# Attention and gated MLP on one core: attention's pieces ahead of erf's batch, and one weight conversion behind the first copy of h

## Chip, cores and metric

The kernel runs on one core of a Trainium2 chip. The metric is the time of one execution on the device in microseconds (us); before the change it is 989.19 us, the median of three runs (986.95 to 989.7).

## What is computed

Linear attention with an RMS norm, followed by a two-layer MLP whose activation is h times erf(softplus(h)):

```python
kv = einsum('bhsd,bhse->bhde', k, v)          # k^T v for every head
out = einsum('bhsd,bhde->bhse', q, kv)
x = out / sqrt(mean(out * out, axis=-1) + 1e-6) * g_norm
h = x @ w_in                                   # x: 4608 x 512, w_in: 512 x 2048
g = h * erf(softplus(h))
result = g @ w_out                             # w_out: 2048 x 512
```

There are 8 batches of 8 heads, 576 rows and 64 columns; the heads of a batch side by side form the 512 columns of x. q, k, v and the result are float32. w_in and w_out come as float64, and the kernel takes their bits apart and makes float32 of them.

## The kernel before

**Groups and steps.** The 4608 rows are cut into nine groups of 512: eight hold 512 rows of one batch each, and the ninth the last 64 rows of all eight. The first two groups (T = 0 and 1) are computed with plain float32 matmuls, while the weights are converted and cut into three parts for the later groups. These go through 16 steps each, one for every 128 columns of w_in (n counts the steps, f is the step within the group). The later groups, from about 275 us on, are not touched by the change.

**A step of the first two groups** issues, in this order: the first list of attention's pieces for the next group (steps[f][0]); a conversion of weights when one is due (weights(): split, join, load); the product of an earlier h with its activation (L584, DVE); four matmuls of h (h_ps, L588, PE; each shows as two records), which take one of two PSUM banks in turn; the copy of h out of PSUM (L599, ACT) and softplus (L600, ACT); in every fourth step erf over the last four tiles (L613, ACT) and a load of softplus's table; the second list of attention's pieces (steps[f][1]); and the product with w_out for the tile five steps back (project, o_ps, L468, PE). Each engine runs its instructions in the order in which they were issued, and waits at the head of its queue until the operands of the next one are there; the order is written out by hand.

**Attention's pieces** for one pair of heads (p = 0 to 3) of the next group: products (k^T v into kv_ps L276 and the transposed q into qt_ps L298 on PE; bd_kv and the tail copied by DVE, L291 and L294; qT copied by ACT, L299); apply (kv_ps L303 and se_ps L304 on PE, then their square by ACT, L307); mean (ms_ps L330 on PE, then Ln, Exp and Square on ACT, L337 to L339, with a load of the table of exp and ln before them and of softplus's after); norm (L345, L348, L357 on DVE). They share two PSUM banks ("at"): kv_ps of a pair takes the bank that L345 of the pair before reads, qt_ps the one that L357 reads. While group 0 is in its steps, products stand in steps 3, 6, 9 and 12, apply in 4, 7, 10 and 13, mean in 5, 8, 11 and 14, all in the second list. Erf's batches stand in steps 3, 7, 11 and 15. While group 1 is in its steps, no piece of the second list falls on a step with erf's batch.

**A conversion** is a split (two DVE instructions, L194 and L203, and two ACT instructions, a relu L202 and an identity L206) and a join (three DVE instructions, L213, L217, L227). Before step 0, attention for group 0 runs in rounds, and w_rounds says which conversions lie between them; a conversion covers two tiles, apart from the first two. The round at the end splits the fifth and sixth tile of w_in (numbers 4 and 5), which are joined in step 2.

Of the kernel before, what the change touches and what calls it, by code (L numbers as in the profile page):

```python
# [28 lines left out]


# [1 line left out]

# [17 lines left out]
BATCH = 4  # L50
# [7 lines left out]
def kernel(  # L58
# [17 lines left out]
    NP = H // 2  # L76
# [24 lines left out]
    def exp_ln_table():  # L101
        nc.scalar.preload_act_table_set("natural_log_exp_and_others")

    def softplus_table():
        nc.scalar.preload_act_table_set("softplus")  # L105
# [131 lines left out]
    def w_next(what):  # L237
        i = w_at[what]
        if i < len(w_order):
            w_at[what] = i + 1  # L240
            {"load": load_w, "split": w_split, "join": w_join}[what](*w_order[i][1:])

    def weights():

        w_next("split")
        w_next("join")
        w_next("load")
# [4 lines left out]
    def attention(T, p, pools=None):  # L252
# [6 lines left out]
        def bank(name):  # L259
            pool, tag = (pools or {}).get(name, (ps_at, "at"))  # L260
            return pool.tile([P, G], FP32, name=name, tag=tag)

        def square_tile(name):

            if T == 0:
                return gate.tile([P, G], FP32, name=name, tag="h")
            return attp.tile([P, G], FP32, name=name, tag="qT")
# [49 lines left out]
            nc.vector.tensor_copy(out=hi, in_=sq)  # L317
            nc.vector.tensor_tensor(out=lo, in0=sq, in1=hi.bitcast(FP32), op=ALU.subtract)

        def mean():  # L320
            ms = st["ms"] = bank("ms_ps")
            if T >= FIRST:


                nc.tensor.matmul(ms, lhsT=mean_w, rhs=st.pop("hi"), start=True, stop=False)
                nc.tensor.matmul(ms, lhsT=mean_w, rhs=st.pop("lo"), start=False, stop=True)
                u = square_tile("u")
            else:
                u = st.pop("qT")
                nc.tensor.matmul(ms, lhsT=mean_f, rhs=u, start=True, stop=True)  # L330
            if T > 0:
                r = attp.tile([P, G], FP32, name="rms_r", tag="rms_r")
                exp_ln_table()
            else:
                r = gate.tile([P, G], FP32, name="rms_r", tag="s")
            st["u"], st["r"] = u, r
            nc.scalar.activation(r, ms, AF.Ln, bias=eps_col)  # L337
            nc.scalar.activation(r, r, AF.Exp, scale=-0.5)
            nc.scalar.activation(u, r, AF.Square)  # L339
            if T > 0 or p == NP - 1:  # L340
                softplus_table()

        def norm():
# [100 lines left out]
    def w_upper(which, f):  # L444

        t = stage.tile([P, 3, G], FP32R, name="w_new", tag="w_new")
        if which == "in":
            x, parts = w_in_sb[:, :, f * P : f * P + P], t.rearrange("p i (c f) -> p i c f", c=KC)
        else:
            x, parts = w_out_sb[:, f, :], t  # L450
        upper_w(x, parts[:, 0])
        w_new[which, f] = t, x, [parts[:, i] for i in range(3)]

    def w_lower(which, f):
        t, x, parts = w_new.pop((which, f))
        lower_w(x, *parts)
        kept = w_kept[which, f] = dram.tile([P, 3, G], FP32, name=f"w_{which}{f}")
        nc.sync.dma_start(out=kept, in_=t.bitcast(FP32))
# [5 lines left out]
    def project(f, g, last):  # L464
        for j in range(J):
            if f == 0:
                o_ps[j] = ps_o.tile([P, DM], FP32, name=f"o_ps{j}", tag=f"o{j}")
            nc.tensor.matmul(  # L468
                o_ps[j],
                lhsT=g[:, j * P : j * P + P],  # L470
                rhs=w_out_sb[:, f, :],
                start=(f == 0),
                stop=last,
            )
# [12 lines left out]
    def sums():  # L487

        for j in range(J):
            e = es[j] = acc.tile([P, DM], FP32, name="e", tag="e")  # L490
            if j % 2:
                nc.scalar.copy(e, o_ps[j])
            else:
                nc.vector.tensor_copy(out=e, in_=o_ps[j])

    def unit(name):
        return gate.tile([P, G], FP32, name=name, tag=name[0])


    for _ in range(2):  # L500
# [7 lines left out]
        2: ("join", "load", "split"),  # L508
        3: ("join", "load"),
        5: ("split",),  # L510
        6: ("join", "load", "split"),
    }
    banks_0 = {"kv_ps": (ps_at, "at"), "qt_ps": (ps_h, "h"), "ms_ps": (ps_h, "h")}
    first = [attention(0, p, banks_0 | {"se_ps": (ps_o, f"o{p}")}) for p in range(NP)]
# [20 lines left out]
    def load_parts(which, n):  # L535

        pool = w_in_p if which == "in" else w_out_p
        for _ in range(n):
            if w_seq[which]:
                key = w_seq[which].pop(0)  # L540
                t = pool.tile([P, 3, G], FP32, name=f"w_{which}_parts", tag="w")
                nc.sync.dma_start(out=t, in_=w_kept[key])
                w_now.setdefault(key, []).append(t)


    def pieces_of(T):


        steps = [([], []) for _ in range(FC)]
        for p in range(NP):  # L550
            products, apply, halve, mean, norm, split = attention(T, p)
            short = T < FIRST or p == NP - 1
            f = (BATCH - 1) * (p + 1) if T < FIRST else BATCH * p
            steps[f][1].append(products)
            steps[f + 1][1].append(apply)
            steps[f + 2][0].append(halve)
            steps[f + 3 - short][short].append(mean)
            steps[f + 4 - short][0].append(norm)
            steps[f + 5 - 2 * short][0].append(split)
        return steps  # L560
# [4 lines left out]
    for n in range(FIRST * FC + 1):  # L565
        T, f = divmod(n, FC)
        if n == FC:
            early_room.close()
            late = ctx.enter_context(tc.tile_pool(name="late", bufs=1))
            x_new = ctx.enter_context(tc.tile_pool(name="x_new", bufs=1))  # L570
            acc = ctx.enter_context(tc.tile_pool(name="acc", bufs=J))
            stage_room = ctx.enter_context(ExitStack())
            stage = stage_room.enter_context(tc.tile_pool(name="stage", bufs=5))
            x_forms[FIRST] = late.tile([P, 3, KC, G], FP32R, name="x_forms0")
        if T < FIRST:
            if f == 0:
                steps = pieces_of(T + 1)
            for piece in steps[f][0]:
                piece()
        while w_at["join"] < len(w_order) and w_order[w_at["join"]][0] <= n + 2:  # L580
            weights()
        done = n - LAG + 1
        if 0 <= done < whole:
            nc.vector.tensor_tensor(out=hs[done], in0=hs[done], in1=ss[done], op=ALU.mult)  # L584
        if T < FIRST:
            h_ps = ps_h.tile([P, G], FP32, name="h_ps", tag="h")
            for c in range(KC):
                nc.tensor.matmul(  # L588
                    h_ps,
                    lhsT=w_in_sb[:, c, f * P : f * P + P],  # L590
                    rhs=xT[T][:, c, :],
                    start=(c == 0),
                    stop=(c == KC - 1),
                )
            if n == whole:
                old_h = wide.tile([P, BATCH, G], FP32, name="h", tag="h")
            h = hs[n] = old_h[:, n - whole] if n >= whole else unit("h_sb")
            s = ss[n] = unit("s_sb")
            nc.scalar.copy(h, h_ps)  # L599
            nc.scalar.activation(s, h, AF.Softplus)  # L600
            for key in list(w_new):
                w_lower(*key)
            if T == FIRST - 1:
                for key in to_cut[:2]:
                    w_upper(*key)
                if not w_new and stage_room is not None:
                    stage_room.close()
                    stage_room = None
                    w_in_p = ctx.enter_context(tc.tile_pool(name="w_in_p", bufs=BATCH))
                    load_parts("in", BATCH)  # L610
            if f % BATCH == BATCH - 1:
                for i in range(n - BATCH + 1, n + 1):
                    nc.scalar.activation(ss[i], ss[i], AF.Erf)  # L613
                softplus_table()
            for piece in steps[f][1]:
                piece()
            if T == FIRST - 1:
                for key in to_cut[2:3]:
                    w_upper(*key)
                del to_cut[:3]  # L620
        if n >= LAG:
            T2, f2 = divmod(n - LAG, FC)
            last = n - LAG in (FC - 1, whole - 1)
            project(f2, hs[n - LAG], last)
            if last:
                sums()
                if T2 == 0:
                    for j in range(J):
                        store(T2, j, es.pop(j))
# [41 lines left out]
    for m in range(first_batch, batches + 1):  # L671
        T, b = divmod(m, NB)
# [7 lines left out]
        def piece():  # L680
            if todo:
                todo.pop(0)()
# [79 lines left out]
```

## Time and profile before

| | before |
|---|---|
| time, median of 3 | 989.19 us |
| span of the profiled execution | 985.3 us |
| PE busy | 947.6 us (96%) |
| DVE busy | 732.9 us (74%) |
| ACT busy | 618.1 us (63%) |
| ACT table loads | 45, 57.7 us |
| DMA, mean rate | 264 GB/s |
| PE waits for DMA v_sb at L276, at the start | 7.8 us in three waits |

PE is TensorE's matmuls, PEld its weight loads, DVE VectorE, ACT ScalarE, SP SyncE, which issues most transfers. The page gives busy shares over the whole span; the waits view adds up the idle time of an engine by what ended it; the timeline lists instructions in order of time; the chain of waits goes back from the last instruction to what released it. The granted clock of PE is 1.00 where PE runs at full speed. A busy share says little where stages have different limits: what a moved instruction is worth is read at the wait that ends last in its stage.

### The profile page before, as it was taken

To read this page: it belongs to the slowest core of one execution; us is meant where nothing else is said; L and a number is where in the kernel's file an instruction comes from. 1 tells how busy PE (TensorE), PEld (TensorE's weight loads), DVE (VectorE), ACT (ScalarE), POOL (GpSimd) and SP (SyncE) were. 2 spreads that over 40 slices of the span, in tenths; PEclk is the share of its full clock that TensorE was granted. 3 is DMA by queue.
4 is the path that set the end of the run, shared out by engine and by line. 5 is a ranking of instruction groups with operands and counts; after the bars stand their busy time and mean duration, and the time that the engine had idled before them with its cause. 6 is when DMAs were issued, how large, how long until landed. Compare 5 with 4: busy or idle time off the path is not lost.

```text
span 985.3 us, 11734 instructions
## 1 busy us (share of the span) xinstructions
PE 947.6 (96%) x4328; PEld 679.1 (69%) x4328; DVE 732.9 (74%) x1039; ACT 618.1 (63%) x822; POOL 2.4 (0%) x10
## 2 busy tenths in 40 slices
PE   6799899999999999999999999999999999989996
PEld 4344444444477877787778787878787787768885
DVE  3987675766367777787777777788777788786666
ACT  4888665777465666666666666666666666665550
POOL 0000000000000000000000000000000000000000
PEclk9999999999999999999999999999999999999999
DMA  9855405888379985998699878988796679667942
GB/s 277 251 179 180 142 17 217 311 353 331 128 269 348 379 281 201 323 360 298 223 278 369 302 263 254 370 297 279 239 339 246 246 258 347 238 229 286 364 199 75
DMA packets 100936, 259.76 MB, mean 264 GB/s; under 512 B 44048, under 2 KB 57360, under 8 KB 100880
## 3 DMA queue, kind: packets, MB, share of 16 engines
q1 hardware_dynamic: 99248, 256.73, 73.3%
q10 hardware_dynamic: 1568, 2.29, 0.8%
q8 instruction: 34, 0.56, 0.2%
q14 instruction: 22, 0.18, 0.1%
q0 software_dynamic: 64, 0.00, 0.0%
HBM read 224.40 MB, written 34.60 MB: 263 GB/s over the span
## 4 chain that ended last, share of the span: by engine, by line
PE 76%; DVE 14%; ACT 6%; DMA 2%; issue 2%; SPq 0%; DVEq 0%
PE n_ps L431 33%; PE m_ps L431 16%; PE h_ps L588 9%; PE o_ps L468 9%; DVE h L724 3%; PE se_ps L304 3%; DVE e L416 2%; PE qt_ps L298 2%; PE kv_ps L276 1%; DVE x L357 1%; DVE u L348 1%; DVE e L411 1%; DVE h L416 1%; DVE u L345 1%; DMA w_raw<-in_moe_w_in_dram 1%
## 5 line engine op out<-in xcount | busy, mean ns | idle before, releaser
L431 PE MATMUL n_ps<-x_forms,w_in_parts 128*128 128x512 f32 x896 | 233.3, 402 | 3.0 <-ACT x_forms L382 2.7
L431 PE MATMUL n_ps<-w_out_parts,g_forms 128*128 128x512 f32 x928 | 232.7, 393 | 3.3 <-DMA w_out_parts<-w_out 3.3
L431 PEld LDWEIGHTS n_ps<-w_out_parts,g_forms 128*128 128x128 f32 x928 | 175.2, 189 | 41.5 <-DMA w_out_parts<-w_out 4.5
L431 PEld LDWEIGHTS n_ps<-x_forms,w_in_parts 128*128 128x128 f32 x896 | 166.6, 188 | 47.3 <-issue 9.1
L708 ACT ACTIVATE s<-h 128x512 f32<-128x512 f32 x112 | 71.1, 635 | 200.3 <-DVE h L416 200.3
L431 PE MATMUL m_ps<-w_out_parts,g_forms 128*128 128x512 f32 x464 | 125.2, 392 | 0.0
L588 PE MATMUL h_ps<-xT,w_in_sb 128*128 128x512 f32 x256 | 115.2, 593 | 5.1 <-ACT h_sb L599 2.2
L431 PE MATMUL m_ps<-x_forms,w_in_parts 128*128 128x512 f32 x448 | 120.0, 390 | 0.0
L416 DVE TENSOR_TENSOR h<-m_ps,h 128x512 f32<-128x512 f32 x112 | 77.1, 688 | 50.5 <-ACT h L706 47.1
L385 DVE TENSOR_TENSOR g_forms<-h,g_forms 128x1024 fp32r<-128x1024 f32 x58 | 70.9, 1223 | 47.0 <-ACT g_forms L382 46.7
L468 PE MATMUL o_ps<-w_out_sb,h_sb 128*128 128x512 f32 x224 | 101.8, 598 | 0.0
L431 PEld LDWEIGHTS m_ps<-w_out_parts,g_forms 128*128 128x128 f32 x464 | 88.1, 190 | 18.6
L431 PEld LDWEIGHTS m_ps<-x_forms,w_in_parts 128*128 128x128 f32 x448 | 84.1, 188 | 17.6
L588 PEld LDWEIGHTS h_ps<-xT,w_in_sb 128*128 128x128 f32 x256 | 48.3, 190 | 65.7 <-issue 56.2
L416 DVE TENSOR_TENSOR e<-m_ps,e 128x512 f32<-128x512 f32 x116 | 80.3, 692 | 17.5 <-PE m_ps L431 9.6
L411 DVE SCALAR_TENSOR_TENSOR e<-n_ps,e 128x512 f32<-128x512 f32 x88 | 60.3, 685 | 27.4 <-PE n_ps L431 27.4
L468 PEld LDWEIGHTS o_ps<-w_out_sb,h_sb 128*128 128x128 f32 x224 | 42.6, 193 | 50.7 <-issue 49.1
L706 ACT ACTIVATE h<-n_ps 128x512 f32<-128x512 f32 x112 | 65.6, 585 | 17.1 <-PE n_ps L431 17.0
L386 DVE SCALAR_TENSOR_TENSOR g_forms<-g_forms 128x1024 fp32r<-128x1024 f32 x58 | 71.1, 1225 | 2.0
L382 ACT ACTIVATE g_forms<-h 128x1024 fp32r<-128x1024 f32 x58 | 61.2, 1055 | 7.8 <-DVE h L724 6.4
L724 DVE TENSOR_TENSOR h<-h,s 128x1024 f32<-128x1024 f32 x56 | 65.9, 1219 | 0.0
L105 ACT ACT_TABLE_LOAD x45 | 57.7, 1283 | 0.8
(81 smaller groups left out, 946.4 us busy)
## 6 DMA issues: line engine op xcount, KB each, us to landing
w_out_parts<-w_out SPq DMA_DIRECT2D x116, 768.0 KB, 7.7
w_in_parts<-w_in SPq DMA_DIRECT2D x112, 768.0 KB, 6.4
w_in<-w_new SPq DMA_DIRECT2D x16, 768.0 KB, 5.6
w_out<-w_new SPq DMA_DIRECT2D x16, 768.0 KB, 6.4
k_sb<-in_k_dram SPq DMA_DIRECT2D x29, 288.0 KB, 5.0
v_sb<-in_v_dram SPq DMA_DIRECT2D x29, 288.0 KB, 5.3
q_sb<-in_q_dram SPq DMA_DIRECT2D x32, 256.0 KB, 5.6
w_raw<-in_moe_w_out_dram SPq DMA_DIRECT2D x8, 1024.0 KB, 5.4
```

Of the source, the lines that this page charges most:

```text
L105: nc.scalar.preload_act_table_set("softplus")
L382: nc.scalar.activation(high, x, AF.Copy, scale=1.0 + 2.0**-13)
L385: nc.vector.tensor_tensor(out=low, in0=x, in1=high.bitcast(FP32), op=ALU.subtract)
L386: nc.vector.scalar_tensor_tensor(out=both, in0=low.bitcast(FP32), scalar=SHIFT, in1=high.bitcast(FP32), op0=ALU.mult, op1=ALU.add,)
L411: nc.vector.scalar_tensor_tensor(out=out_, in0=ps, scalar=scale, in1=out_, op0=ALU.mult, op1=ALU.add)
L416: nc.vector.tensor_tensor(out=out_, in0=ps, in1=out_, op=ALU.add)
L431: nc.tensor.matmul(ps, lhsT=weights(form, k), rhs=moving(form, k), start=(form == forms[0] and k == 0), stop=(form == forms[-1] and k == 3),)
L468: nc.tensor.matmul(o_ps[j], lhsT=g[:, j * P : j * P + P], rhs=w_out_sb[:, f, :], start=(f == 0), stop=last,)
L588: nc.tensor.matmul(h_ps, lhsT=w_in_sb[:, c, f * P : f * P + P], rhs=xT[T][:, c, :], start=(c == 0), stop=(c == KC - 1),)
L706: nc.scalar.activation(h[:, i], n_ps, AF.Copy, scale=SHIFT - 1.0)
L708: nc.scalar.activation(s[:, i], h[:, i], AF.Softplus)
L724: nc.vector.tensor_tensor(out=h[:, part], in0=h[:, part], in1=s[:, part], op=ALU.mult)
```

## The change

In the first two groups a step's second list of attention's pieces is issued ahead of erf's batch instead of behind it, so that what PE and DVE wait for does not stand behind erf and its table loads on ACT. Where a mean falls on a step of erf's batch, the load of softplus's table at its end is left out, since erf's table follows at once. The split of the fifth and sixth tile of w_in goes from the last round before step 0 to a place behind the copy and softplus of step 0, so that ACT does not hold the first copy of h behind it.

```diff
-        def mean():
+        def mean(table=True):
...
-            if T > 0 or p == NP - 1:
+            if table and (T > 0 or p == NP - 1):
                 softplus_table()
...
-        6: ("join", "load", "split"),
+        6: ("join", "load"),
...
-            steps[f + 3 - short][short].append(mean)
+            with_erf = short and (f + 2) % BATCH == BATCH - 1
+            steps[f + 3 - short][short].append(partial(mean, table=not with_erf))
...
+            if n == 0:
+                w_next("split")
+            for piece in steps[f][1]:
+                piece()
             if f % BATCH == BATCH - 1:
                 for i in range(n - BATCH + 1, n + 1):
                     nc.scalar.activation(ss[i], ss[i], AF.Erf)
                 softplus_table()
-            for piece in steps[f][1]:
-                piece()
```

In the order of the instructions PE, DVE and SP are the same in both kernels. On ACT the relu and identity of tiles 4 and 5 go behind the first copy and softplus; the qT copy (L299) of step 3, the square (L307) of step 7 and the mean (L337 to L339) of step 11 go ahead of erf's batch; one table load is gone.

## The prediction

> **What bounds the kernel now.** I read the page first: PE is busy 947.6 of 985.3 us, and 76% of the chain that ended last is PE. So the question is where PE stands still, and whether the change reaches those places. The waits of PE, from the waits view (engine, line, tile, what it waited for: us in total, times, longest):
>
> ```profile
> PE kv_ps L276 <- DVE qT L345: 2.5, 1, 2.5
> ...
> PE h_ps L588 <- ACT h_sb L599: 2.2, 1, 2.2
> PE h_ps L588 <- DVE xT L357: 2.0, 1, 2.0
> PE se_ps L304 <- ACT qT L299: 1.6, 1, 1.6
> PE kv_ps L303 <- DVE bd_kv L291: 1.4, 1, 1.4
> ```
>
> Apart from the xT line, these are single waits that an instruction named by the diff stands behind. The timeline of PE around the largest (start us, us, engine, line, operation; the bracket is the idle time ahead and its releaser):
>
> ```profile
> 111.26 3.60 PE L588 MATMUL h_ps<-xT,w_in_sb 128*128 128x512 f32 x8
> 117.31 0.92 PE L276 MATMUL kv_ps<-v_sb,k_sb 96*64 96x64 f32 x24 [2.45 <-DVE qT L345]
> 118.82 1.10 PE L298 MATMUL qt_ps<-ident,q_sb 128*128 128x128 f32 x4 [0.59 <-DVE xT L357]
> 119.72 4.88 PE L468 MATMUL o_ps<-w_out_sb,h_sb 128*128 128x512 f32 x8
> 124.43 3.60 PE L588 MATMUL h_ps<-xT,w_in_sb 128*128 128x512 f32 x8
> 129.42 0.43 PE L303 MATMUL kv_ps<-qT_last,bd_kv 128*128 128x64 f32 x2 [1.39 <-DVE bd_kv L291]
> ```
>
> PE stops three times, and its eight o_ps records take 4.88 us instead of 3.60. The timeline of ACT just before shows what DVE's L345 waited for:
>
> ```profile
> 107.17 0.59 ACT L599 COPY h_sb<-h_ps 128x512 f32<-128x512 f32 x1 [2.38 <-PE h_ps L588]
> 107.79 0.63 ACT L600 ACTIVATE s_sb<-h_sb 128x512 f32<-128x512 f32 x1
> 108.44 1.28 ACT L613 ACT_TABLE_LOAD   x1
> 109.73 2.19 ACT L613 ACTIVATE s_sb<-s_sb 128x512 f32<-128x512 f32 x4
> 111.94 1.28 ACT L105 ACT_TABLE_LOAD   x1
> 113.23 1.28 ACT L102 ACT_TABLE_LOAD   x1
> 114.52 0.69 ACT L337 ACTIVATE rms_r<-ms_ps,eps_col 128x512 f32<-128x512 f32 x1
> 115.24 0.63 ACT L338 ACTIVATE rms_r<-rms_r 128x512 f32<-128x512 f32 x1
> 115.90 0.63 ACT L339 ACTIVATE qT<-rms_r 128x512 f32<-128x512 f32 x1
> ```
>
> The mean of the third pair (step 11) waits behind erf's batch and two table loads; only then does the chain L345, weight conversion, L291 on DVE start, without a gap up to 129.38. Last, the stretches after it (us; then busy time and instructions of PE, PEld, DVE, ACT, POOL; granted clock; DMA share; GB/s):
>
> ```profile
> 130.00:230.00 100.00, 100.00 (x316) 46.46 (x315) 69.76 (x113) 67.02 (x102) 0.00 (x0) 1.00 0.63 241
> 230.00:275.00 45.00, 45.00 (x156) 20.96 (x154) 18.79 (x31) 30.36 (x43) 0.00 (x0) 1.00 0.51 197
> 275.00:985.00 710.00, 693.71 (x3414) 558.39 (x3410) 549.67 (x757) 428.91 (x558) 0.00 (x0) 1.00 0.79 283
> ```
>
> From 130 to 275 us PE never stops, so whatever PE gains by 130 us is carried to the end.
>
> **What the Trainium skill says.** "ScalarE: Activation LUTs", What ACT_TABLE_LOAD costs: 1.28 us for the load and 1.38 us of drain, 2.66 in all. The trace agrees with the load (1.28) but shows no drain: the Ln starts 0.01 us after the load ends. I take 1.28. The same page, Table sets: copies, relu and identity are in every set. The trace agrees: the copies of L599 and the relu of L202 run under softplus's table without a load, and so does the Square of L307. Moving L299 and L307 ahead of erf therefore adds no load. "TensorE: Matmul & The Clock Gate", What's actually happening: an idle window of some 3.4 us halves PE's clock. The trace shows half clock (0.50) from 119.1 to 122.1 us, after 2.45 and 0.59 us of idle time; after single gaps of 1.99 and 2.17 us the clock stayed at 1.00.
>
> **The change, part by part.** In the two kernels' instruction order PE, DVE and SP are identical. On ACT four things move, all in the first group (in the second group no piece falls on a step of erf), and one table load goes.
>
> Step 0: before, the relu and identity of tiles 4 and 5 stand ahead of the first copy of h. ACT is idle for 4.40 us until 38.01, then runs these two, and copies h only at 40.01, though h's first tile was ready at about 34.8 (33.90 plus two records of 0.43). PE stops from 38.46 to 40.63 for that bank. Now the copy and softplus lie inside ACT's idle stretch. PE's third tile starts at 38.46: w_in's tiles 2 and 3 are written by 36.14 + 1.23 = 37.37, and the second bank's copy comes at 40.0, ahead of its need at 41.9. PE gains 2.17. ACT, busy without a break from 38.01, gains the copy's and softplus's slot, 41.14 - 40.01 = 1.13, and the 0.20 that it waited for the fourth tile (47.80): 1.33. DVE is unmoved; L194 there follows other DVE work.
>
> Step 3: the qT copy (L299, 0.59) stands ahead of two table loads and erf (1.28 + 2.19 + 1.28). It comes at about 49.06 - 1.33 = 47.7 instead of 53.87, with its transposes ready at 49.3 - 2.17 = 47.1. se_ps then waits for nothing: bd_kv and the tail are done by 49.0. PE would have gained 2.17 + 1.60 = 3.77 and be at the mean's matmul (L330) at 58.91 - 3.77 = 55.14. But that needs the Square (L307) of step 4, which stays behind erf's batch; it ended at 58.08 and now ends at 58.08 - 1.33 = 56.75. **A new wait** of 1.6 us at L330, behind which o_ps is queued on PE, takes part of the gain: L330 starts at 56.8, a gain of 2.11.
>
> From there to step 11 PE keeps 2.11 and ACT and DVE keep 1.33. The tightest place is qt_ps at 67.57 - 2.11 = 65.46 against L357 ending at 66.76 - 1.33 = 65.43; all banks and joins I followed have over 0.5 us to spare.
>
> Step 7: the Square moves from 81.27 to about 75.1, ahead of erf; se_ps is ready at about 74.1, so ACT does not wait. The mean that uses it was bound by PE (82.89) and stays so. Worth nothing on PE: the o_ps and h_ps matmuls hide it.
>
> Step 11: h's copy waits for PE, so it comes at 107.17 - 2.11 = 105.06. Then softplus, the exp table (106.33 to 107.61), and Ln at once, as ms_ps is ready at 107.83 + 0.86 - 2.11 = 106.6. Before, 114.52 - 108.44 = 6.08 lay between softplus and Ln; now 1.28. That is 4.80 us, erf and two loads. With 2.11, L345 starts at 116.56 - 6.91 = 109.65. Erf's batch now ends at about 113.1 instead of 111.92, but its first user (L584 of step 12) is on DVE at about 121. ACT is free for step 12's relu at 114.4; its result is needed at 124.75 - 6.9 = 117.85. So DVE's chain moves whole, and L291 ends at 129.38 - 6.9 = 122.5. PE no longer stops at kv_ps and qt_ps (112.6 and 113.4, against L345 and L357 ending at 110.4 and 111.9), and runs o_ps and h_ps up to 120.75. It waits 1.7 us for L291 instead of 1.39, and L303 starts at 129.42 - 6.9 = 122.5.
>
> Sum: 2.11 + 4.80 = 6.9 us, and 989.2 - 6.9 = 982.3.
>
> **The rivals.**
> Clock loss: the new waits of 1.6 and 1.7 us let the clock fall as at 119.1. Before, that cost 4.88 - 3.60 = 1.28 and 1.10 - 0.66 = 0.44, hidden behind DVE; now 1.7 would be on the path, giving 984.0. Against it: gaps of 1.99 and 2.17 us did not do so.
> No early gain: PE loses the 2.11 between steps 4 and 11, since ACT, with some 48 of 60 us busy there, becomes what it waits for. Left are 4.8 us, 984.4; with the clock loss too, 986.1. Against it: the tight places above hold.
> More gain: the Square of step 4 does not delay L330, and PE keeps 3.77: 8.6 us, 980.6. It needs ACT 1.6 us faster than the sum of its rows.
> Slower: work that now comes earlier meets the transfers otherwise, and the last stretch (DMA share 0.79, PE idle 16.3 us of 710) waits more. To end slower than before by 3 us, these 16.3 would have to grow by 9.9: 992. Against it: stores and loads there are paced by PE's own steps, and a shift leaves their spacing alone.
>
> **How the numbers follow.** Main case 0.68 (982.3; its three timed runs may scatter as those of before, 986.95 to 989.7), clock loss or no early gain 0.20 (984 to 986.1), more gain 0.06 (980.6), slower or nothing 0.06. The range takes in all but the last and the outer scatter: 979.8 to 986.0. Faster by over 0.3% (under 986.2): 0.89; the same 0.07; slower 0.04.
>
> **What would show it.** Right: no wait of h_ps for h_sb, of se_ps for qT or of kv_ps for qT L345; a new wait of ms_ps L330 for qT of about 1.6 us; kv_ps L303 still waiting about 1.7 us; 44 table loads instead of 45; ACT's Ln of step 11 some 1.3 us after its softplus; PE full from 123 us on. Wrong: half clock after 122 us, or PE waits in the later stretches that were not there.

## The result, and the profile after

The changed kernel took 980.24 us (median of four runs, 977.81 to 981.87) beside 989.4 us for the kernel before (median of four, 986.95 to 989.7): ratio 0.9911, 95% interval 0.9885 to 0.9937. The forecast was 982.3 in a range of 979.8 to 986.0. The spans of the profiled executions are 985.3 and 978.7 us, 6.6 apart.

The interval lies below 1: the change is faster, and PE's waits are the ones named beforehand. The waits view of the kernel after (line numbers are one to six higher: L308 is the square of L307, L331 the mean's matmul of L330, L304 the kv_ps of L303, L292 the copy of L291, L619 the erf of L613):

```profile
PE h_ps L590 <- DVE xT L358: 2.0, 1, 2.0
PE ms_ps L331 <- ACT qT L308: 1.7, 1, 1.7
PE kv_ps L304 <- DVE bd_kv L292: 1.5, 1, 1.5
```

The waits for the first copy of h, for the qT copy and for L345 of the third pair are gone; the one at the mean's matmul is new; the one at bd_kv stayed. PE's timeline around step 12 of the kernel after (start us, us, engine, line, operation; in brackets the idle time ahead):

```profile
109.57 3.60 PE L590 MATMUL h_ps<-xT,w_in_sb 128*128 128x512 f32 x8
113.09 0.92 PE L277 MATMUL kv_ps<-v_sb,k_sb 96*64 96x64 f32 x24
113.94 0.66 PE L299 MATMUL qt_ps<-ident,q_sb 128*128 128x128 f32 x4
114.44 3.60 PE L469 MATMUL o_ps<-w_out_sb,h_sb 128*128 128x512 f32 x8
117.87 3.60 PE L590 MATMUL h_ps<-xT,w_in_sb 128*128 128x512 f32 x8
122.94 0.43 PE L304 MATMUL kv_ps<-qT_last,bd_kv 128*128 128x64 f32 x2 [1.47 <-DVE bd_kv L292]
```

Of three stops one is left, and o_ps takes 3.60 us again. ACT ahead of it, in the timeline of the kernel after:

```profile
105.47 0.59 ACT L601 COPY h_sb<-h_ps 128x512 f32<-128x512 f32 x1 [1.73 <-PE h_ps L590]
106.09 0.63 ACT L602 ACTIVATE s_sb<-h_sb 128x512 f32<-128x512 f32 x1
106.74 1.28 ACT L103 ACT_TABLE_LOAD   x1
108.03 0.69 ACT L338 ACTIVATE rms_r<-ms_ps,eps_col 128x512 f32<-128x512 f32 x1
108.75 0.63 ACT L339 ACTIVATE rms_r<-rms_r 128x512 f32<-128x512 f32 x1
109.42 0.63 ACT L340 ACTIVATE qT<-rms_r 128x512 f32<-128x512 f32 x1
110.06 1.28 ACT L619 ACT_TABLE_LOAD   x1
111.36 2.19 ACT L619 ACTIVATE s_sb<-s_sb 128x512 f32<-128x512 f32 x4
```

From the table load after softplus to Ln it is 108.03 - 106.74 = 1.29 us; before it was 6.08. Erf has moved behind the mean. The page counts 44 loads of softplus's table instead of 45. (The 45 in the table above are this line's alone; over all lines it is 114 loads of tables before and 113 after.) And the stretches of the kernel after that follow (us; busy time of PE, PEld, DVE, ACT, POOL; granted clock; DMA share; GB/s):

```profile
123.00:223.00 100.00, 100.00 (x317) 46.64 (x318) 69.69 (x112) 66.62 (x102) 0.00 (x0) 1.00 0.62 239
223.00:268.00 45.00, 45.00 (x143) 20.75 (x143) 18.82 (x31) 30.28 (x43) 0.00 (x0) 1.00 0.52 202
268.00:978.00 710.00, 693.92 (x3432) 559.02 (x3428) 550.06 (x758) 429.10 (x559) 0.00 (x0) 0.99 0.79 283
```

They are those of before, shifted: PE full for 145 us, then 693.92 of 710 busy, against 693.71.

A span carries the scatter of the start, where the first transfers land, and of PE's clock. Of the seventeen runs of before that stand beside the first experiments, the five above 989 us had a granted clock of 0.992 over the whole run, the seven below 987 us one of 0.994 or 0.995. So the runs below are read by a **yardstick** inside one trace: from the h_ps record of step 0 that waited for xT (33.90 us before, 34.47 after; 33.44 to 35.72 over all traces) to kv_ps of the last pair (129.42 and 122.94). It begins with these records in PE's timeline, before:

```profile
33.90 4.56 PE L588 MATMUL h_ps<-xT,w_in_sb 128*128 128x512 f32 x10 [1.99 <-DVE xT L357]
40.63 7.13 PE L588 MATMUL h_ps<-xT,w_in_sb 128*128 128x512 f32 x16 [2.17 <-ACT h_sb L599]
```

and after, where the wait for the first copy of h is gone:

```profile
34.47 11.43 PE L590 MATMUL h_ps<-xT,w_in_sb 128*128 128x512 f32 x26 [1.99 <-DVE xT L358]
```

Before the yardstick is 95.52 us, after 88.47: the change is worth 7.05 us there. (The expectations call that record the fifth; it is the seventh.)

| kernel | yardstick, us | less than before | time, us (runs) | ratio to before, 95% |
|---|---|---|---|---|
| before | 95.52 | | 989.4 (4); beside the others 987.52, 986.11, 987.62 | |
| after | 88.47 | 7.05 | 980.24 (4) | 0.9911, 0.9885 to 0.9937 |
| after, again | 88.45 | 7.07 | 979.59 (6) | 0.9934, 0.9921 to 0.9947 |
| split alone | 94.75; again 94.73 | 0.77; 0.79 | 987.0 (12); again 988.03 (1) | 0.9994, 0.9981 to 1.0007 |
| pieces alone | 90.42 | 5.10 | 982.69 (6) | 0.9947, 0.9929 to 0.9965 |
| step 11 alone | 90.73 | 4.79 | 982.25 (4) | 0.9943, 0.9923 to 0.9963 |
| after, table load kept | 88.46 | 7.06 | 979.06 (1) | |
| after, late conversion | 86.83; again 86.84 | 8.69; 8.68 | 977.0 (4); again 978.49 (6) | 0.9911, 0.9897 to 0.9925; 0.9912, 0.9894 to 0.993 |
| after, step 4's split late | 88.36 | 7.16 | 979.34 (1) | |
| after, all three late | 84.85; again 86.55 | 10.67; 8.97 | 977.18 (5); again 976.37 (5) | 0.9908, 0.9896 to 0.9921; 0.9894, 0.9879 to 0.9909 |

### The profile page after: what moved, and what is told of

Read it like the earlier page. It is cut to its first block, busy times and chain, and to the rows that moved or that the text cites. A ratio compares the mean times of both kernels' runs of the same rounds, so it can differ in the third digit from the quotient of the medians.

```text
span 978.7 us, 11733 instructions
## 1 busy us (share of the span) xinstructions
PE 945.3 (97%) x4328; PEld 678.4 (69%) x4328; DVE 732.6 (75%) x1039; ACT 616.1 (63%) x821; POOL 2.4 (0%) x10
## 4 chain that ended last, share of the span: by engine, by line
PE 79%; DVE 13%; ACT 5%; DMA 2%; issue 1%; DVEq 0%
PE n_ps L432 35%; PE m_ps L432 17%; PE o_ps L469 9%; PE h_ps L590 8%; PE se_ps L305 3%; DVE h L728 3%; DVE e L417 2%; PE qt_ps L299 2%; PE kv_ps L277 2%; DVE x L358 1%; DVE u L349 1%; DVE e L412 1%; DVE u L346 1%; DVE h L417 1%; PE ms_ps L327 1%
```

## The experiments

**The size of it: the changed kernel again.** No edit; it was timed again, in more runs.

> The changed kernel once more, without any edit, timed in more rounds. Theory: the traces differ by 7.05 us between step 0 and the last pair's kv_ps, and nothing after it; 6.9 us less than before, ratio 0.993. Rival (the later stretches gain too, as the first comparison of times with 9.2 us might be read): 9 us or more, ratio 0.991 or less.

The ratio is 0.9934, 6.5 us less than before, and the yardstick is 88.45. The first comparison's 9.2 us came from few runs of before, three of four near 989.5 us, where the medians beside the later runs are 986.1 to 987.6. The rival, that the later stretches gain too, asked for a ratio of 0.991 or less, and the interval lies above that (the first one, from four runs each, had not ruled it out). The traces agree: from the yardstick's end to the end of the span it is 855.9 us before, and 855.8 and 854.6 in the two traces of the changed kernel, with a granted clock of 0.995, 0.995 and 0.997 over the whole run.

**Step 11 alone**, with its table load left out as in the changed kernel (diff against the kernel before).

```diff
+            if n == 11:
+                for piece in steps[f][1]:
+                    piece()
             if f % BATCH == BATCH - 1:
...
-            for piece in steps[f][1]:
-                piece()
+            if n != 11:
+                for piece in steps[f][1]:
+                    piece()
```

> The kernel before with one edit: only the mean of step 11 goes ahead of erf's batch, with its table load left out; steps 0, 3 and 7 as before. Theory: 4.80 us of ACT's chain (erf 2.2 and two table loads) leave the path of L345, DVE's chain follows whole: 95.52 - 4.80 = 90.7 us, and the waits of PE at steps 2 and 4 (2.2 and 1.6 us) stay. Rival (worth only PE's own idle time and lost clock at kv_ps and qt_ps, 2.45 + 0.59 + 1.7, less what DVE makes it wait again at L303): under 3.5 us, 92 or more.

95.52 - 90.73 = 4.79 us, against 4.80 worked out. In PE's timeline of this kernel the product k^T v and the transposes of step 12 run without a stop, and the one wait left there is that for bd_kv:

```profile
114.76 0.92 PE L277 MATMUL kv_ps<-v_sb,k_sb 96*64 96x64 f32 x24
115.61 0.66 PE L299 MATMUL qt_ps<-ident,q_sb 128*128 128x128 f32 x4
116.10 3.60 PE L469 MATMUL o_ps<-w_out_sb,h_sb 128*128 128x512 f32 x8
119.54 3.60 PE L590 MATMUL h_ps<-xT,w_in_sb 128*128 128x512 f32 x8
124.61 0.43 PE L304 MATMUL kv_ps<-qT_last,bd_kv 128*128 128x64 f32 x2 [1.48 <-DVE bd_kv L292]
```

The rival counted on PE's side and expected PE to wait again for bd_kv. PE did lose its stops of 2.45 and 0.59 us and the 1.28 + 0.44 = 1.72 us of lost clock, 4.76 in all; but the wait for bd_kv hardly grew, from 1.39 to 1.48, because DVE's chain came 4.8 us earlier as a whole (L345 starts 77.86 us into the yardstick instead of 82.66, and bd_kv is copied by 90.68 instead of 95.47). So the two counts agree here. That ACT's chain sets the size, and not PE's clock, is seen in the two traces of the split alone.

**The pieces alone**, with the split of tiles 4 and 5 back in its old place (diff against the changed kernel).

```diff
-        6: ("join", "load"),
+        6: ("join", "load", "split"),
...
-            if n == 0:
-                w_next("split")
```

> The changed kernel with the split of tiles 4 and 5 back ahead of step 0; the three moved pieces and the table load as in the changed kernel. Theory: se_ps no longer waits (1.60), but the mean's matmul then waits about 0.8 us for the square behind erf's batch, so 0.78 is left of it; step 11 gives 4.80: 95.52 - 5.58 = 89.9 us. Rival (every removed wait is kept): 95.52 - 6.40 = 89.1 us.

5.10 us, of which step 11 is 4.79: moving the qT copy of step 3 and the square of step 7 adds 0.31, not 0.78. PE still waits 2.17 us for the first copy of h, so the transposes of step 3 come later than ACT, and the copy, now ahead of erf, waits for them. In ACT's and PE's timelines of this kernel:

```profile
48.88 0.58 ACT L300 COPY qT<-qt_ps 128x512 f32<-128x512 f32 x1 [0.29 <-PE qt_ps L299]
```

```profile
58.05 1.12 PE L331 MATMUL ms_ps<-qT,mean_f 128*128 128x512 f32 x2 [1.26 <-ACT qT L308]
```

These 0.29 us go into ACT's sum up to the square, and the mean's matmul waits 1.26 us instead of the 0.8 expected. A moved piece can put a new wait at its new place. In the changed kernel the copy has no such wait (47.96 us, without a bracket), as the split's move brings the transposes earlier.

**The split alone** (diff against the kernel before).

```diff
-        6: ("join", "load", "split"),
+        6: ("join", "load"),
...
+            if n == 0:
+                w_next("split")
             if f % BATCH == BATCH - 1:
```

> The kernel before with one edit: the split of tiles 4 and 5 goes behind the first copy of h; the pieces stay behind erf's batch. Yardstick for these runs: from the fifth record onward of step 0's h_ps (the one that waits for xT, 33.90 us before) to the last pair's kv_ps L303 (129.42): 95.52 us before, 88.47 in the changed kernel. Theory: ACT gains 1.33 us, PE gains 2.17 at first but se_ps of step 4 still waits for the qT copy behind erf, so that only ACT's 1.33 is left: 94.2 us, no wait of h_ps for h_sb, and a wait of se_ps for qT of about 2.4. Rival (every removed wait of PE is kept): 93.35 us. Half clock near kv_ps as before.

> The split alone once more, as the first look had 1.69 us of half clock inside its 26 records of h_ps, just where the yardstick begins (13.12 us for them instead of 11.43). Theory as there: with PE at full clock at that place the yardstick is 94.2 us and se_ps waits some 2.4 us for the qT copy. Rival: the split alone is worth 0.8 us whatever the clock, 94.75.

Both traces give 0.8 us, and se_ps waits 1.6 us for the qT copy, not 2.4. But in both PE fell to half clock just where the yardstick begins (13.12 us for the 26 records in each). PE's timeline and the stretches of the second trace:

```profile
34.08 13.12 PE L588 MATMUL h_ps<-xT,w_in_sb 128*128 128x512 f32 x26 [1.99 <-DVE xT L357]
53.94 1.13 PE L304 MATMUL se_ps<-qT,bd_kv 128*128 128x512 f32 x2 [1.59 <-ACT qT L299]
```

```profile
34.10:37.50 3.40, 3.40 (x4) 1.38 (x5) 3.37 (x4) 1.22 (x2) 0.00 (x0) 0.52 0.94 351
```

The 26 records take 13.12 us instead of the 11.43 in the kernel after, 1.69 more. The wait for the first copy of h is gone, as worked out; what it gave PE was mostly lost to the clock, and ACT's third and fourth copies then waited for PE (0.20 us in brackets each). The split alone was not seen at a full clock there, so its size is not measured. An estimate comes from the changed kernel, whose ACT has the same order up to the fourth copy of h: this copy starts 46.82 - 34.47 = 12.35 us into the yardstick, in the two traces of the split alone at 13.15 and 13.16, and before at 13.90. By that the half clock took 0.8 us from ACT, and without it the split alone would give about 0.8 + 0.8 = 1.6 us. Beside the pieces it gives more, 7.05 - 5.10 = 1.95.

The two traces also show what PE's clock is worth ahead of the wait for bd_kv. In PE's timeline of the first:

```profile
120.80 4.41 PE L468 MATMUL o_ps<-w_out_sb,h_sb 128*128 128x512 f32 x8
130.47 0.43 PE L303 MATMUL kv_ps<-qT_last,bd_kv 128*128 128x64 f32 x2 [1.83 <-DVE bd_kv L291]
```

and of the second:

```profile
118.75 3.60 PE L468 MATMUL o_ps<-w_out_sb,h_sb 128*128 128x512 f32 x8
128.81 0.44 PE L303 MATMUL kv_ps<-qT_last,bd_kv 128*128 128x64 f32 x2 [3.03 <-DVE bd_kv L291]
130.18 5.11 PE L468 MATMUL o_ps<-w_out_sb,h_sb 128*128 128x512 f32 x8
```

With half clock or without it the yardstick is the same, 94.75 and 94.73 us: what PE saves there it waits for bd_kv, at the end of the chain through ACT and DVE. Behind that wait nothing hides it: in the second trace half clock came after the 3.03 us, and o_ps took 5.11 us instead of 3.60.

**The table load that was left out**, put back (diff against the changed kernel).

```diff
-            steps[f + 3 - short][short].append(partial(mean, table=not with_erf))
+            steps[f + 3 - short][short].append(partial(mean, table=True))
```

> The changed kernel with the load of softplus's table at the end of step 11's mean put back (45 loads instead of 44). Theory: what counts is that the mean stands ahead of erf; the load left out is worth nothing there, as ACT's next work is first needed by DVE's second join at 118.26 and has over a us to spare: 88.5 us as in the changed kernel, ACT's relu of step 12 some 1.28 later. Rival: the table load is on the path, 89.7 us.

88.46 us: leaving it out was worth nothing on the yardstick, and PE is busy without a gap from its end to 270 us here too. ACT's timeline of this kernel, with two loads side by side and the relu of step 12 late:

```profile
109.43 1.28 ACT L106 ACT_TABLE_LOAD   x1
110.71 1.28 ACT L619 ACT_TABLE_LOAD   x1
112.01 2.19 ACT L619 ACTIVATE s_sb<-s_sb 128x512 f32<-128x512 f32 x4
114.22 1.28 ACT L106 ACT_TABLE_LOAD   x1
115.51 1.15 ACT L203 ACTIVATE w_e<-w_e,exp_col 128x1024 int32<-128x1024 int32 x1
```

The relu starts 115.51 - 33.84 = 81.67 us into the yardstick instead of 114.86 - 34.47 = 80.39, 1.28 later, and DVE never waits for it. So the 4.79 us of step 11 come from the place of the mean.

**Is the new wait at the mean's matmul what limits now?** The split of step 4 goes behind that step's pieces, so the square comes earlier (diff against the changed kernel; weights(False) leaves the split out).

```diff
-            weights()
+            weights(n != 4)
...
+            if n == 4:
+                w_next("split")
```

> The changed kernel with the split of step 4 (out tiles 2 and 3) behind that step's pieces, so that the square L308 comes 2.1 us earlier on ACT. Theory: the new wait of the mean's matmul for qT (1.72 us) goes, but ACT's sum up to the norm is the same, so PE waits at kv_ps and qt_ps of step 6 for L346 and L358 instead (0.9 and 0.7 us): 88.3 us, 0.1 less than the changed kernel. Rival (the wait at the mean's matmul is the limit, as the waits view has it): 88.47 - 1.72 = 86.75 us.

88.36 us, 0.1 less than the changed kernel. PE's timeline of this kernel (L332 is the mean's matmul of L330, L347 and L359 are L345 and L357):

```profile
55.21 1.02 PE L332 MATMUL ms_ps<-qT,mean_f 128*128 128x512 f32 x2
56.07 3.60 PE L470 MATMUL o_ps<-w_out_sb,h_sb 128*128 128x512 f32 x8
59.51 3.60 PE L591 MATMUL h_ps<-xT,w_in_sb 128*128 128x512 f32 x8
64.26 0.92 PE L278 MATMUL kv_ps<-v_sb,k_sb 96*64 96x64 f32 x24 [1.16 <-DVE qT L347]
65.78 0.66 PE L300 MATMUL qt_ps<-ident,q_sb 128*128 128x128 f32 x4 [0.59 <-DVE xT L359]
```

The wait at the mean is gone, and 1.16 + 0.59 = 1.75 us stand at the next two places that hang on ACT. The waits view shows where PE stopped first, not how much would be won there: behind it lay ACT's sum up to the norm.

**The wait for bd_kv.** The second of step 12's two weight conversions goes behind that step's pieces (diff against the changed kernel).

```diff
-        while w_at["join"] < len(w_order) and w_order[w_at["join"]][0] <= n + 2:
+        due = sum(1 for w in w_order[w_at["join"]:] if w[0] <= n + 2)
+        late_w = due - 1 if n == 12 else 0
+        for _ in range(due - late_w):
             weights()
...
             for piece in steps[f][1]:
                 piece()
+            for _ in range(late_w):
+                weights()
```

> The changed kernel with the second of step 12's two weight conversions behind the pieces of that step, so that bd_kv (L292 there) stands ahead of it on DVE. Theory: the wait of kv_ps L304 for bd_kv, 1.47 us, is all that this conversion costs, and goes: 88.47 - 1.47 = 87.0 us, PE full from there on. Rival: the copies or the products of later steps wait in its place, 88.5 us.

88.47 - 86.83 = 1.64 us less: the wait of 1.47, and 0.17 by which records that follow without a wait overlap (117.97 + 3.60 = 121.57, and kv_ps starts at 121.40). PE's timeline of this kernel, without a bracket:

```profile
117.97 3.60 PE L592 MATMUL h_ps<-xT,w_in_sb 128*128 128x512 f32 x8
121.40 0.33 PE L304 MATMUL kv_ps<-qT_last,bd_kv 128*128 128x64 f32 x2
```

**All three late**: this conversion, and the splits of steps 4 and 5 behind their pieces, so that the norm comes earlier as well. The diff is against the kernel with step 4's split late; the late conversion is as above.

```diff
-            weights(n != 4)
+            weights(n not in (4, 5))
...
-            if n == 4:
+            if n in (4, 5):
                 w_next("split")
```

> The changed kernel with the splits of steps 4 and 5 behind those steps' pieces, and the second conversion of step 12 behind its pieces. Theory: now the norm of step 6 ends some 2 us earlier, so PE keeps the 1.72 us that it waited at the mean, and the 1.47 of bd_kv: 88.47 - 3.19 = 85.3 us, no idle time of PE between step 0 and the later stretches, 3.2 us less than the changed kernel. Rival: splits that come later make the joins of steps 5 and 6, and through them PE, wait: 87 us or more.

84.85 us, 3.62 less than the changed kernel, and PE does not stop from step 0 up to 264 us, in the stretches of this kernel:

```profile
34.16:134.16 100.00, 100.00 (x339) 46.76 (x340) 87.82 (x111) 80.75 (x103) 0.00 (x0) 1.00 0.50 162
134.16:264.00 129.84, 129.84 (x422) 60.52 (x422) 76.52 (x128) 87.49 (x132) 0.00 (x0) 1.00 0.66 254
```

Yet its time, 977.18 us, was that of the kernel with the late conversion alone, 977.0. So both were run once more, side by side:

> The second conversion of step 12 behind its pieces, once more, beside the next kernel on the same chip. By its trace 1.6 us less than the changed kernel, if the clock takes its breaks at the same places.

> The splits of steps 4 and 5 too, once more, beside the kernel before it. By the traces PE is 2.0 us further at the last pair's kv_ps and still 2.3 us ahead at 806 us. Theory: the equal times of the first comparison came from half clock in the last 150 us, at other places in every run, and over five rounds it is 1 to 2 us faster than the one before it. Rival: the later stretches take the 2.0 us back, and the two are within 0.5 us.

976.37 against 978.49 us, 2.1 apart, but the two intervals of the ratio overlap, and the first pair had shown no difference: in time the two are not told apart. By the first traces the kernel with all three stays ahead up to 830.52 against 832.83 us (the same ms_ps record in both; 0.41 of it comes from the start), and loses it in half clock near 835 us and after the wait for w_out near 958 us, which the other trace does not have. In its second trace it loses 1.69 us to half clock in step 0 (yardstick 86.55) and has such stretches again within 830 to 840 and 960 to 970 us (0.83 granted over each). With two traces of each kernel it stays open whether that is chance or comes with the kernel. The later stretches do not take the gain back by waiting: from 270 us to the end PE is idle for 16.9 to 17.4 us in the four traces of the two kernels, and for 16.6 us before. Both kernels beat the one before. The one with all three also beats the changed kernel: timed on one chip beside the same runs of before, its five runs took 976.0 to 977.52 us, and the six of the changed kernel 977.56 to 981.33.

## Why the prediction was right

The sum and the waits that it rests on came as forecast. By its steps, each against the trace after (starts taken from 33.90 and 34.47):

- **Step 0**, third tile without a wait: right; the 26 records of h_ps run in one piece of 11.43 us. ACT's gain of 1.33 measured 1.59: the square of step 4 ended 24.18 us in before and 22.59 after, in ACT's timelines:

```profile
57.50 0.58 ACT L307 ACTIVATE qT<-se_ps 128x512 f32<-128x512 f32 x1
```

```profile
56.48 0.58 ACT L308 ACTIVATE qT<-se_ps 128x512 f32<-128x512 f32 x1
```

The term was mis-sized: the wait of ACT for PE at the fourth tile, 0.20 in brackets, had shifted ACT's start there by 0.29 (46.56 to 47.80, against 45.87 to 46.82 after), and one at the third tile, without a bracket, by 0.11.

- **Step 3 and the new wait**: right. Predicted 1.6 us at the mean's matmul and a gain of 2.11 for PE; measured 1.72 and (58.91 - 33.90) - (57.11 - 34.47) = 2.37, in PE's timelines before and after:

```profile
54.51 1.13 PE L304 MATMUL se_ps<-qT,bd_kv 128*128 128x512 f32 x2 [1.60 <-ACT qT L299]
58.91 1.02 PE L330 MATMUL ms_ps<-qT,mean_f 128*128 128x512 f32 x2
```

```profile
57.11 1.13 PE L331 MATMUL ms_ps<-qT,mean_f 128*128 128x512 f32 x2 [1.72 <-ACT qT L308]
```

That the wait caps PE because of ACT's sum is shown by the run with step 4's split late. The tightest place, qt_ps of step 6, had 0.03 us to spare by the prediction's sum and has 65.88 - 65.73 = 0.15 in the trace.

- **Step 7**, worth nothing on PE: the square starts at 75.36, and the mean's matmul at 81.19 has no wait, as said. It was not undone by itself, but with the qT copy of step 3 it gave 0.31 us in all.
- **Step 11**, 4.80: 4.79 alone, with the table load left out worth nothing in that place. The 4.80 are erf and the two loads that no longer stand ahead of Ln; that one load less is run adds nothing. Ln did wait in ACT's order and not for PE: its ms_ps was ready at 106.97 + 1.02 = 107.99 us before, and Ln started at 114.52. (The prediction has ms_ps ready at 106.6, from 107.83 + 0.86, and so counts 0.86 us twice; by the line of L330 it is 105.9. Ln waits for its table until 107.61 either way.)
- **The wait for L291** was put at 1.7 and is 1.47; full PE from 123 us on, and one load of softplus's table less, are there.
- **The sum** was 6.9, measured 7.05 on the yardstick: 2.27 at the copy of h in step 11 (73.27 against 71.00 us in), and 4.79 from there, less rounding. The time itself came 2.1 us under the forecast, mostly since the base of 989.2 was high: with the later medians of before, 986.1 to 987.6, less 6.9, one gets 979.2 to 980.7. That the time fell 0.44 us inside the lower end of the range is in part luck, and one of its four runs lies below it; what bears the sum out is the yardstick.
- **The clock rival**: no half clock came at 122 us. But the argument against it, that gaps of 1.99 and 2.17 us had left the clock alone, was too firm: after gaps of 0.9 and 1.99 us it fell in both traces of the split alone and in one of the last kernel. It then costs 1.7 us of PE's time, as that rival had it, only at another place; and in the second trace of the split alone it fell at the rival's own place, after a wait of 3.03 us. In the second trace of the changed kernel it fell just ahead of the yardstick, where the wait for xT hid it. That it stayed off the path in both traces of the changed kernel is luck as far as the runs show.
- **No early gain** and **slower** did not happen; **more gain** (3.77) needs ACT's work up to the norm of step 6 to end earlier. The last kernel shows it: with the splits of steps 4 and 5 late PE does not stop there.

## What to carry to other kernels

Where two engines feed each other in order, price a moved instruction by the chain that it leaves (erf and two table loads ahead of the mean, 4.8 us), and then walk on to the next place where the same engine is waited for: freeing PE at one wait moved 1.75 us to the next two. Edits on one chain are not additive, so undo them one by one. For a gain of a few us among runs that scatter as much, measure between two events in the trace rather than from the whole time.

## What the runs showed of the hardware

PE's half-clock stretches came at different places in executions of one kernel, each costing up to 1.7 us: in step 0 in some traces (0.83 granted over 30 to 40 us in the second trace of the split alone), near 840, 865 or 885 us in others, and near 960 after a wait of 2.8 to 3.0 us for w_out. The Trainium skill, "TensorE: Matmul & The Clock Gate", What's actually happening, says that the window over which activity is counted runs freely; that agrees with the changing places, though no run here shows the window itself. The prediction quotes an idle window of some 3.4 us ahead of half clock. Here it came without a single gap of that length: in the first trace of the split alone half clock came after gaps of 1.28, 0.94 and 1.99 us, while after the 3.01 us for w_out in the first trace with the late conversion the clock stayed at 1.00. So the length of one gap does not tell whether the clock falls.

The wait for the first copy of h, 2.17 us, would have hidden such a stretch, by an estimate from the lines of before: 38.46 + 1.69 = 40.15 us, ahead of the 40.63 at which PE went on. Half clock fell into step 0 in eight of the ten traces with the moved split. In five of them it lay in the six records ahead of the yardstick, and the wait for xT shrank from 1.99 us to 0.3 or 0.5 instead; in three it lay in the 26 records behind, and came onto PE's path. In the three traces without the moved split it did not fall there. Why stays open: up to there the order of ACT's work is the same.
